# First x block in three loads, the gate row's product in bank 0, second-layer weights in three loads

## The chip, the cores and the metric

The kernel runs on one core of one Trainium2 chip. A core has a matrix engine (TensorE, PE in the profile; its weight loads are PEld), VectorE (DVE), ScalarE (ACT), GpSimd (POOL) and SyncE (SP), which here issues nearly all DMAs; sixteen DMA engines move the data. Matrix products go to PSUM, eight banks of 512 fp32 columns per partition, and are copied from there to SBUF by VectorE or ScalarE. The metric is the device time of one execution in microseconds, lower being better.

## The reference

The inputs are bf16. With S = 2048 tokens, D = 512, 32 heads of 16, and a hidden width of 1376:

```python
x = A_x
g = sigmoid((x * gate_w).sum(-1, keepdims=True))
# branch A: linear attention with softmax feature maps
q, k, v = split_heads(x @ wqkv)                    # 32 heads of 16
pq, pk = q @ w_phi[h], k @ w_phi[h]
phi = lambda p: concat([softmax(p), softmax(-p)])  # 32 features per head
kv = einsum("bhsf,bhsd->bhfd", phi(pk), v)
z  = phi(pk).sum over s
a  = ((phi(pq) @ kv) / (phi(pq) @ z + 1e-6)) @ wo
# branch B: two dense layers
b  = relu(x @ w1) @ w2
return g * a + (1 - g) * b
```

## The kernel before

**How order is made.** The program is written as one list of operations per engine (`_Plan`). Each operation may name events it waits for (`after`) and one event that it sets (`ev`); `emit` turns these into semaphore waits and increments, in the order of the list. Each engine works through its list in order. `early(eng)` marks a point in a list: what was listed before it is placed ahead of that engine's wait at the start barrier. SP's x loads, ACT's load of the gate row, DVE's two memsets and some of TensorE's warm-up products are placed so.

**Banks.** `free[bank]` holds the event that says when a PSUM bank was last read out; whoever writes the bank next waits for it. `nextbank()` deals out banks 3, 4 and 5 in turn. `gatecol` (L223) is given its bank by the caller (L562), which computes the same number as `nextbank()` would without advancing the turn.

**The start.** The first 512 tokens are loaded by `loadx0` into `XS`, four token rows per partition, so that index j = 0..3 stands for 128 tokens each. `xtr` (L235) turns 128x128 blocks (feature block dt, token block j) by a product with the identity into a PSUM bank, and `xev` (L244) copies a bank to the transposed x, `XT`, on DVE or ACT. Groups are named: a0, a1, a2 hold the feature blocks 0, 1 and 2 to 3 of the first half of the tokens, c0 and d0 feature block 0 of j = 2 and j = 3, b1 and b3 the rest of the second half. Ahead of them `warm` issues products of ones whose result nobody reads. SP then loads the first-layer weights W1 by feature block: block 0 in two pieces, blocks 1, 2 and 3 whole, and the remaining columns for all blocks (`w1r`); then the small feature-map weights, the v weights WV, and DMA transposes of the q and k weights and of the other x blocks.

`slab(t)` (L520) does feature block t of the first eight hidden units for the first 512 tokens: eight products of 512 columns, one in each PSUM bank, accumulated over the four slabs. A slab waits for its W1 piece and for the x groups that `XV[t]` names. ReLUs on ACT and DVE empty the banks. Two more hidden units (`hunit`), then `gatecol(...)`, `vtile(0)`, `vtile(1)` and the eight `pre(i)` follow, where `pre` multiplies the q and k weights with the feature map. `gatecol` transposes the gate row into a column, which DVE copies into a spare column of W1 (the event `gw`); `rest` reads that column with the last hidden units.

**The middle and the end.** For each of 16 token tiles, `atile` computes the feature map arguments, ACT the exponentials, DVE and GpSimd the normalisation; `kv` accumulates the key-value product three tiles later, and hidden units of later token blocks are put in between. The second-layer weights W2 are loaded at tile 3 (L591 to L595), on one semaphore. Afterwards, per tile, `nd` multiplies with the key-value product, `finB` (L485) does the second dense layer, `finA` the output projection, and `comb` (L508) mixes the two and stores.

Of the kernel before, what the change touches and what calls it, by code (L numbers as in the profile page):

```python
# [68 lines left out]
def bass_gated_mix__linear_kernel_hedgehog__dense_activation_relu__prompt_kernel(  # L69
# [17 lines left out]
    P = 128  # L87
# [14 lines left out]
    KU = KT - 1  # L102
    NR = DFF - KU * P

    with ExitStack() as es:
# [37 lines left out]
        XS = OT[:, 0, :].rearrange("p (j d) -> p j d", j=4)  # L143
# [7 lines left out]
        p = _Plan(["sp", "pool", "act", "dve", "pe"])  # L151
        free = {b: [] for b in range(8)}


        xq = x2[0:512, :].rearrange("(p j) d -> p j d", j=4)
        oq = o2[0:512, :].rearrange("(p j) d -> p j d", j=4)

        def orow(m):
            return oq[:, m, :] if m < 4 else o2[m * P:(m + 1) * P, :]

        def loadx0(h):
            p.dma("sp", lambda e: e.dma_start(out=XS[:, 2 * h:2 * h + 2, :], in_=xq[:, 2 * h:2 * h + 2, :]),
                  f"x0{h}", ev=f"x0{h}")

        def loadw1(t, c0=0, c1=DFF, tag=""):
            p.dma("sp", lambda e: e.dma_start(  # L166
# [2 lines left out]
        p.dma("act", lambda e: e.dma_start(out=GR[0:NDT, :], in_=gate_w.rearrange("(j p) -> j p", p=P)),  # L169
              "gr", after=["grz"], ev="gr")  # L170
        p.early("act")
        for h in range(2):
            loadx0(h)
        p.early("sp")
        loadw1(0, 0, 4 * P, "a")
# [1 line left out]
        for t in range(1, NDT):  # L177
            loadw1(t, 0, 8 * P)
        p.dma("sp", lambda e: e.dma_start(
            out=W1[:, :, 8 * P:DFF], in_=B_w1[:, 8 * P:DFF].rearrange("(j p) n -> p j n", p=P)), "w1r", ev="w1r")  # L180
        p.dma("sp", lambda e: e.dma_start(
            out=WPS[:, :, :], in_=A_w_phi.rearrange("(g hl) r c -> (hl r) g c", g=NDT)), "wps", ev="wps")
        p.dma("sp", lambda e: e.dma_start(
            out=WV[:, :, :], in_=A_wqkv[:, 2 * D:3 * D].rearrange("(j p) n -> p j n", p=P)), "wv", ev="wv")
        for i in range(2):
            p.dma("sp", lambda e, i=i: e.dma_start_transpose(
                out=WQKT[:, 4 * i:4 * i + 4, :], in_=A_wqkv[:, i * D:(i + 1) * D]), f"wqk{i}", ev=f"wqk{i}")
        for c in range(1, NCH):
            p.dma("sp", lambda e, c=c: e.dma_start_transpose(
                out=XT[:, :, c * 512:(c + 1) * 512], in_=x2[c * 512:(c + 1) * 512, :]), f"x{c}", ev=f"x{c}")  # L190
# [9 lines left out]
            after=["wps"], ev="wd")  # L200
        for gt in range(NDT):
# [4 lines left out]
                after=["wd", "m8"], ev=f"wbd{gt}")  # L206
# [5 lines left out]
             after=["iota0"], ev="idn")  # L212
        p.op("dve", lambda e: e.tensor_single_scalar(ROW8[:, :], ROW8[:, :], 4, ALU.arith_shift_right),
             after=["iota"], ev="r8")
# [3 lines left out]
             after=["r64"], ev="m32")  # L218
# [4 lines left out]
        def gatecol(bank):  # L223
            gp = PS[:, bank, 0:NDT]
            p.op("pe", lambda e: e.matmul(gp, GR[:, :], IDN[:, 0:NDT], start=True, stop=True),  # L225
                 after=["gr", "idn"] + free[bank], ev="gp")
            p.op("dve", lambda e: e.tensor_copy(W1[:, :, DFF:DFF + 1], gp.unsqueeze(2)), after=["gp"], ev="gw")  # L227
            free[bank] = ["gw"]

        def warm(n, cols=512):  # L230
            for _ in range(n):
                p.op("pe", lambda e: e.matmul(PS[:, 4, 0:cols], ones[:, 0:P], ones[:, 0:cols], start=True, stop=True),
                     after=["one"])

        def xtr(nm, js, dts, bank, last=True, off=0):  # L235
            blocks = [(dt, j) for dt in dts for j in js]
            for i, (dt, j) in enumerate(blocks):
                o = off + i * P
                p.op("pe", lambda e, dt=dt, j=j, o=o: e.matmul(
                    PS[:, bank, o:o + P], XS[:, j, dt * P:(dt + 1) * P], IDN[:, :], start=True, stop=True),  # L240
                    after=["idn", f"x0{j // 2}"] + (free[bank] if o == 0 else []),
                    ev=(f"xt{nm}" if last and i == len(blocks) - 1 else None))

        def xev(eng, nm, js, dts, bank):  # L244
            w = len(js) * P
            d = XT[:, dts[0]:dts[-1] + 1, js[0] * P:js[0] * P + w]
            s = PS[:, bank, 0:len(dts) * w].rearrange("p (t c) -> p t c", c=w)
            if eng == "dve":
                p.op("dve", lambda e: e.tensor_copy(d, s), after=[f"xt{nm}"], ev=f"xv{nm}")
            else:  # L250
                p.op("act", lambda e: e.activation(d, s, ACT.Copy), after=[f"xt{nm}"], ev=f"xv{nm}")
            free[bank] = [f"xv{nm}"]
# [12 lines left out]
        rot = [0]  # L265
# [5 lines left out]
        def hunit(c, kt, eng="act", bank=None):  # L271
            bank = nextbank() if bank is None else bank
            for t in range(NDT):
                p.op("pe", lambda e, t=t: e.matmul(  # L274
                    PS[:, bank, :], W1[:, t, kt * P:(kt + 1) * P], XT[:, t, c * 512:(c + 1) * 512],
                    start=(t == 0), stop=(t == NDT - 1)),
                    after=(xready(c) + w1all + free[bank] if t == 0 else ()),
                    ev=(f"h{c}_{kt}" if t == NDT - 1 else None))
            relu(c, kt, bank, eng)
# [123 lines left out]
        def vtile(m, eng="act", bank=2):  # L403
            b = m % VB
            for dt in range(NDT):
                p.op("pe", lambda e, dt=dt: e.matmul(  # L406
                    PS[:, bank, :], XT[:, dt, m * P:(m + 1) * P], WV[:, dt, :],
                    start=(dt == 0), stop=(dt == NDT - 1)),
                    after=((xready(m // 4) + ["wv"] + free[bank]) if dt == 0 else ()),
                    ev=(f"v{m}" if dt == NDT - 1 else None))  # L410
            dst, src = VS[:, b, :, 0:64], PS[:, bank, :].rearrange("p (g c) -> p g c", g=NG)
            after = [f"v{m}"] + ([f"kv{m - VB}"] if m >= VB else [])
            if eng == "dve":
                p.op("dve", lambda e: e.tensor_copy(dst, src), after=after, ev=f"cv{m}")
            else:
                p.op("act", lambda e: e.activation(dst, src, ACT.Copy), after=after, ev=f"cv{m}")  # L416
            free[bank] = [f"cv{m}"]

        def kv(m):
            b = m % NB  # L420
            vb = m % VB
            for g in range(NG):
                after = []
                if g == 0:
                    after = [f"pk{m}", f"cv{m}", f"one{vb}"]
                    if m == 0:
                        after += free[6] + free[7]
                p.op("pe", lambda e, g=g: e.matmul(  # L428
                    PS[:, 6 + g // 4, (g % 4) * GW:(g % 4) * GW + 65],
                    EB[:, b, 3, g * P:(g + 1) * P], VS[:, vb, g, 0:65],  # L430
                    start=(m == 0 and g % 4 == 0), stop=(m == NT - 1), skip_group_check=True),
                    after=after, ev=(f"kv{m}" if g == NG - 1 else None))
# [93 lines left out]
                    ev=(f"h0_{u}" if t == NDT - 1 else None))  # L526

        A, B = (0, 1), (2, 3)
        warm(5)
        p.early("pe")  # L530
        warm(1, 384)
        xtr("a0", A, (0,), 6)
        xtr("a1", A, (1,), 5)
        xtr("a2", A, (2,), 7, last=False)
        xtr("c0", (2,), (0,), 2)
        xtr("d0", (3,), (0,), 0)
        xtr("a2", A, (3,), 7, off=2 * P)
        xev("dve", "a0", A, (0,), 6)
        xev("act", "c0", (2,), (0,), 2)
        xev("dve", "d0", (3,), (0,), 0)  # L540
        xev("act", "a2", A, (2, 3), 7)
        xev("dve", "a1", A, (1,), 5)
        xtr("b1", B, (1, 2), 1)
        xtr("b3", B, (3,), 6)
        xev("act", "b1", B, (1, 2), 1)
        xev("dve", "b3", B, (3,), 6)
        slab(0)
# [11 lines left out]
            relu(0, u, UB[u], ("act", "dve")[u % 2])  # L559
        hunit(0, 8)  # L560
        hunit(0, 9, "dve")
        gatecol(3 + rot[0] % 3)  # L562
        vtile(0, "dve")
        vtile(1, "act", nextbank())
        for i in range(4):
# [10 lines left out]
        def unit(c, k):  # L576
            if k < 0:
                rest(c)
            else:
                hunit(c, k)  # L580

        for m in range(NT):
            atile(m)
            if m >= LAG:
                kv(m - LAG)
            if m + 3 < NT:
                vtile(m + 3)
            for u in mid[m]:
                unit(*u)
            if m == 3:  # L590
                for a, b in ((0, 4), (4, 7), (7, KU)):  # L591
                    p.dma("sp", lambda e, a=a, b=b: e.dma_start(
                        out=W2[:, a:b, :], in_=B_w2[a * P:b * P, :].rearrange("(j p) n -> p j n", p=P)),
                        "w2", ev=f"w2{a}")
                p.dma("sp", lambda e: e.dma_start(out=W2[0:NR, KU, :], in_=B_w2[KU * P:DFF, :]), "w2", ev="w2")  # L595
            if m == 5:
                for a in range(0, NDT, 2):
                    p.dma("sp", lambda e, a=a: e.dma_start(
                        out=WO[:, a:a + 2, :], in_=A_wo[a * P:(a + 2) * P, :].rearrange("(j p) n -> p j n", p=P)),
                        "wo", ev="wo" if a else None)  # L600
# [69 lines left out]
```

The softmax here doesn't subtract the row's maximum and nothing guards it: scores larger than these inputs give would overflow.

## Time and profile before

| | |
|---|---|
| median of 6 runs | 147.36 us (147.13 to 147.74) |
| the profiled execution, its own time | 147.17 us |
| its span, first to last instruction | 145.9 us |
| PE busy | 143.3 us (98%), 978 products |
| DVE busy | 92.4 us (63%) |
| ACT busy | 72.8 us (50%) |
| POOL busy | 52.1 us (36%) |
| DMA | 16.12 MB, mean 111 GB/s |

The profile page gives busy time per engine, the span in 40 slices, the DMA queues, the chain of work that ended last (followed back from the last instruction through what released each step), the costliest groups of instructions, and the DMA issues. Other views of the trace list waits by who waited for whom, one line's instructions, the instructions in order of time, and busy time within chosen stretches. An L number is a line of the kernel; times are microseconds from the start of the span unless marked ns. Products on TensorE are pipelined and their ends are modelled, so starts are the safer reading. "SPq" is SP issuing a DMA; landing is when the data's last semaphore update came.

### The profile page before, as it was taken

Reading aid. Unit: us, or ns where it says so; the run is one execution under the profiler, and the core shown is the slowest. Engines: PE = TensorE matmul, PEld = TensorE weight load, DVE = VectorE, ACT = ScalarE, POOL = GpSimd, SP = SyncE. Lnnn points to the kernel's source line nnn. Section 1 sums busy time; section 2 is a strip of 40 time slices with the busy share of each in tenths; the row PEclk is TensorE's granted clock in tenths of the full one; section 3 lists DMA queues with packets and bytes.
Section 4 is the critical chain, followed back from the end, with each engine's and each line's share of the span. In section 5 each row is a group of like instructions: output and inputs, shape, how many; then the busy total and the mean of one; then the engine's idle time right before and its main releaser. Section 6 shows DMA issues by size and latency. Waiting matters only on the chain.

```text
span 145.9 us, 2539 instructions
## 1 busy us (share of the span) xinstructions
PE 143.3 (98%) x978; PEld 72.9 (50%) x978; DVE 92.4 (63%) x158; ACT 72.8 (50%) x125; POOL 52.1 (36%) x62
## 2 busy tenths in 40 slices
PE   8999999999999999999999999999999999999994
PEld 3444754444446455544645555554444444444442
DVE  3528728777687878678698967664445555554342
ACT  3316567789778778797878862022211111111150
POOL 2022003778868678688869810200000000000000
PEclk9999999999999999999999999999999999999999
DMA  6999995113349983325834431354332223222213
GB/s 189 277 250 203 228 172 120 31 41 76 72 89 366 127 211 81 71 62 108 75 75 88 91 72 40 73 108 126 83 82 73 72 72 76 72 72 74 72 45 106
DMA packets 45221, 16.12 MB, mean 111 GB/s; under 512 B 39352, under 2 KB 44568, under 8 KB 45208
## 3 DMA queue, kind: packets, MB, share of 16 engines
q1 hardware_dynamic: 45056, 15.92, 50.2%
q8 instruction: 8, 0.13, 0.4%
q10 hardware_dynamic: 152, 0.03, 0.1%
q14 instruction: 5, 0.04, 0.1%
HBM read 4.41 MB, written 2.10 MB: 45 GB/s over the span
## 4 chain that ended last, share of the span: by engine, by line
PE 94%; DMA 3%; DVE 1%; SPq 1%; issue 0%
PE PS L485 26%; PE PS L274 19%; PE PS L330 18%; PE PS L406 10%; PE PS L494 9%; PE PS L522 4%; DMA W<-in_B_w_dram 3%; PE PS L460 3%; PE PS L428 3%; PE PS L286 2%; PE PS L308 1%; DVE WQK L508 1%; SPq L166 1%; PE PS L225 0%
## 5 line engine op out<-in xcount | busy, mean ns | idle before, releaser
L485 PE MATMUL PS<-W,HT 128*128 128x512 bf16 (+4 forms) x187 | 40.6, 366 | 0.0
L374 POOL TENSOR_TENSOR EB<-EB,SC 128x1024 bf16<-128x1024 bf16 x15 | 28.9, 1928 | 23.6 <-DVE SC L372 23.6
L350 ACT ACTIVATE EB<-PS 128x480 bf16<-128x480 f32 (+1 forms) x44 | 30.1, 756 | 14.2 <-PE PS L330 14.2
L499 ACT ACTIVATE TFA<-PS,GT 128x512 bf16<-128x512 f32 x16 | 11.0, 687 | 42.7 <-PE PS L494 36.6
L274 PE MATMUL PS<-XT,W 128*128 128x512 bf16 x128 | 30.7, 379 | 0.0
L330 PE MATMUL PS<-WQK,XT 128*128 128x480 bf16 x128 | 28.5, 366 | 0.0
L370 DVE TENSOR_REDUCE ZB<-EB 128x64 f32<-128x1024 bf16 x15 | 18.3, 1220 | 14.2 <-ACT EB L350 14.2
L508 DVE SCALAR_TENSOR_TENSOR WQK<-PS,OMG,TFA 128x512 bf16<-128x512 f32 (+2 forms) x17 | 12.2, 719 | 23.6 <-ACT TFA L499 22.4
L485 PEld LDWEIGHTS PS<-W,HT 128*128 128x128 bf16 (+1 forms) x187 | 17.0, 98 | 17.4
L260 ACT ACTIVATE HT<-PS 128x512 bf16<-128x512 f32 x35 | 20.3, 614 | 7.0 <-PE PS L522 5.1
L330 PEld LDWEIGHTS PS<-WQK,XT 128*128 128x128 bf16 x128 | 12.5, 98 | 13.6
L385 DVE TENSOR_REDUCE ZB<-EB 128x64 f32<-128x1024 bf16 x16 | 18.7, 1167 | 0.0
L274 PEld LDWEIGHTS PS<-XT,W 128*128 128x128 bf16 x128 | 12.0, 98 | 13.2
L394 POOL TENSOR_TENSOR EB<-EB,SC 128x512 bf16<-128x512 bf16 x16 | 16.9, 1058 | 1.3
L406 PE MATMUL PS<-WV,XT 128*128 128x512 bf16 x64 | 16.4, 378 | 0.0
L494 PE MATMUL PS<-WO,OT 128*128 128x512 bf16 x64 | 16.1, 378 | 0.0
L470 DVE TENSOR_TENSOR WQK<-PS,RDEN 128x512 bf16<-128x512 f32 x16 | 11.1, 691 | 0.6
L494 PEld LDWEIGHTS PS<-WO,OT 128*128 128x128 bf16 x64 | 6.1, 97 | 7.2
L416 ACT ACTIVATE VS<-PS 128x512 bf16<-128x512 f32 x14 | 8.5, 608 | 2.2 <-PE PS L406 2.2
L372 DVE RECIPROCAL SC<-ZB 128x64 f32<-128x64 f32 x16 | 8.8, 553 | 0.5
L406 PEld LDWEIGHTS PS<-WV,XT 128*128 128x128 bf16 x64 | 5.4, 97 | 5.0 <-DVE W L227 0.5
L460 PEld LDWEIGHTS PS<-KVNZ,PHQ 128*128 128x128 bf16 x128 | 6.1, 97 | 3.6
(57 smaller groups left out, 87.6 us busy)
## 6 DMA issues: line engine op xcount, KB each, us to landing
out_dram<-WQK SPq DMA_DIRECT2D x15, 128.0 KB, 1.7
W<-in_B_w_dram SPq DMA_DIRECT2D x3, 256.0 KB, 5.2
W<-in_B_w_dram SPq DMA_DIRECT2D x2, 384.0 KB, 5.5
OT<-in_A_x_dram SPq DMA_DIRECT2D x2, 256.0 KB, 2.9
WV<-in_A_wqkv_dram SPq DMA_DIRECT2D x1, 512.0 KB, 6.7
W<-in_B_w_dram SPq DMA_DIRECT2D x1, 512.0 KB, 4.3
WO<-in_A_wo_dram SPq DMA_DIRECT2D x2, 256.0 KB, 3.6
W<-in_B_w_dram SPq DMA_DIRECT2D x1, 352.0 KB, 6.2
```

The source lines that it names most:

```text
L260: p.op("act", lambda e: e.activation(dst, src, ACT.Relu), after=[f"h{c}_{kt}"], ev=ev)
L274: p.op("pe", lambda e, t=t: e.matmul(PS[:, bank, :], W1[:, t, kt * P:(kt + 1) * P], XT[:, t, c * 512:(c + 1) * 512], start=(t == 0), stop= ...
L330: p.op("pe", lambda e, dt=dt, which=which: e.matmul(PS[:, which, 0:DE], XT[:, dt, m * P:(m + 1) * P], WQK[:, which, dt * DE:(dt + 1) * DE] ...
L350: p.op("act", lambda e: e.activation(dst, s_, ACT.Exp, scale=scale), after=[f"qk{m}"] + busy, ev=ev)
L370: p.op("dve", lambda e: e.tensor_reduce(zk, ek, AX.X, ALU.add), after=[emk, f"cst{b}"], ev=f"zk{m}")
L374: p.op("pool" if m < NT - 1 else "dve", lambda e: e.tensor_tensor(EB[:, b, 3, :].rearrange("p (g f) -> p g f", f=DH), EB[:, b, 2, :].rearr ...
L385: p.op("dve", lambda e: e.tensor_reduce(ZB[:, b, 0:64].rearrange("p (h s) -> p h s", s=2), bass.AP(tensor=EB, offset=base, ap=[[EBS, P], [ ...
L394: p.op("pool", lambda e: e.tensor_tensor(EB[:, b, 0, :].rearrange("p (h s f) -> p h s f", h=H, s=2)[:, :, 1, :], EB[:, b, 1, :].rearrange( ...
L406: p.op("pe", lambda e, dt=dt: e.matmul(PS[:, bank, :], XT[:, dt, m * P:(m + 1) * P], WV[:, dt, :], start=(dt == 0), stop=(dt == NDT - 1)), ...
L485: p.op("pe", lambda e, kt=kt, M=M: e.matmul(PS[:, bank, 0:n], HT[0:M, kt, m * P:(m + 1) * P], W2[0:M, kt, cs], start=(kt == 0), stop=(kt = ...
L494: p.op("pe", lambda e, t=t: e.matmul(PS[:, bank, :], OT[:, t, m * P:(m + 1) * P], WO[:, t, :], start=(t == 0), stop=(t == NDT - 1)), after ...
L508: p.op("dve", lambda e: e.scalar_tensor_tensor(out=OSB[:, ob, cs], in0=PS[:, bank, 0:n], scalar=OMG[:, m:m + 1], in1=TFA[:, m % 2, cs], op ...
```

## The change

Four things are edited.

- The x block is loaded in three pieces in place of two: j = 0, j = 1, and j = 2 to 3 (`XJ`; `XP` maps j to its piece). All three are issued ahead of SP's wait at the start barrier.
- `xtr` takes a list of blocks. The first half's transposes are issued in two batches: feature blocks 0, 1, 2 of j = 0, then 0, 1, 2 of j = 1 with feature block 3 of both. The copies of a0 and a1 stand first in DVE's list; c0 and d0 are transposed after all of a2. The warm-up is four products of 512 columns and one of 256 ahead of the transposes, and one of 256 between j = 1 and c0; before, it was five of 512 and one of 384.
- `gatecol` uses bank 0.
- W2's first ten blocks are loaded as 5 + 5 in place of 4 + 3 + 3; the last, partial block stays a load of its own.

```diff
@@ -158,9 +158,12 @@
         def orow(m):
             return oq[:, m, :] if m < 4 else o2[m * P:(m + 1) * P, :]
 
+        XJ = ((0, 1), (1, 2), (2, 4))
+        XP = (0, 1, 2, 2)
+
         def loadx0(h):
-            p.dma("sp", lambda e: e.dma_start(out=XS[:, 2 * h:2 * h + 2, :], in_=xq[:, 2 * h:2 * h + 2, :]),
-                  f"x0{h}", ev=f"x0{h}")
+            j0, j1 = XJ[h]
+            p.dma("sp", lambda e: e.dma_start(out=XS[:, j0:j1, :], in_=xq[:, j0:j1, :]), f"x0{h}", ev=f"x0{h}")
 
         def loadw1(t, c0=0, c1=DFF, tag=""):
             p.dma("sp", lambda e: e.dma_start(
@@ -169,7 +172,7 @@
         p.dma("act", lambda e: e.dma_start(out=GR[0:NDT, :], in_=gate_w.rearrange("(j p) -> j p", p=P)),
               "gr", after=["grz"], ev="gr")
         p.early("act")
-        for h in range(2):
+        for h in range(3):
             loadx0(h)
         p.early("sp")
         loadw1(0, 0, 4 * P, "a")
@@ -232,13 +235,12 @@
                 p.op("pe", lambda e: e.matmul(PS[:, 4, 0:cols], ones[:, 0:P], ones[:, 0:cols], start=True, stop=True),
                      after=["one"])
 
-        def xtr(nm, js, dts, bank, last=True, off=0):
-            blocks = [(dt, j) for dt in dts for j in js]
+        def xtr(nm, blocks, bank, last=True, off=0):
             for i, (dt, j) in enumerate(blocks):
                 o = off + i * P
                 p.op("pe", lambda e, dt=dt, j=j, o=o: e.matmul(
                     PS[:, bank, o:o + P], XS[:, j, dt * P:(dt + 1) * P], IDN[:, :], start=True, stop=True),
-                    after=["idn", f"x0{j // 2}"] + (free[bank] if o == 0 else []),
+                    after=["idn", f"x0{XP[j]}"] + (free[bank] if o == 0 else []),
                     ev=(f"xt{nm}" if last and i == len(blocks) - 1 else None))
 
         def xev(eng, nm, js, dts, bank):
@@ -526,22 +528,25 @@
                     ev=(f"h0_{u}" if t == NDT - 1 else None))
 
         A, B = (0, 1), (2, 3)
-        warm(5)
+        warm(4)
         p.early("pe")
-        warm(1, 384)
-        xtr("a0", A, (0,), 6)
-        xtr("a1", A, (1,), 5)
-        xtr("a2", A, (2,), 7, last=False)
-        xtr("c0", (2,), (0,), 2)
-        xtr("d0", (3,), (0,), 0)
-        xtr("a2", A, (3,), 7, off=2 * P)
+        warm(1, 256)
+        xtr("a0", ((0, 0),), 6, last=False)
+        xtr("a1", ((1, 0),), 5, last=False)
+        xtr("a2", ((2, 0),), 7, last=False)
+        xtr("a0", ((0, 1),), 6, off=P)
+        xtr("a1", ((1, 1),), 5, off=P)
+        xtr("a2", ((2, 1), (3, 0), (3, 1)), 7, off=P)
+        warm(1, 256)
+        xtr("c0", ((0, 2),), 2)
+        xtr("d0", ((0, 3),), 0)
         xev("dve", "a0", A, (0,), 6)
+        xev("dve", "a1", A, (1,), 5)
         xev("act", "c0", (2,), (0,), 2)
         xev("dve", "d0", (3,), (0,), 0)
         xev("act", "a2", A, (2, 3), 7)
-        xev("dve", "a1", A, (1,), 5)
-        xtr("b1", B, (1, 2), 1)
-        xtr("b3", B, (3,), 6)
+        xtr("b1", [(dt, j) for dt in (1, 2) for j in B], 1)
+        xtr("b3", [(3, j) for j in B], 6)
         xev("act", "b1", B, (1, 2), 1)
         xev("dve", "b3", B, (3,), 6)
         slab(0)
@@ -559,7 +564,7 @@
             relu(0, u, UB[u], ("act", "dve")[u % 2])
         hunit(0, 8)
         hunit(0, 9, "dve")
-        gatecol(3 + rot[0] % 3)
+        gatecol(0)
         vtile(0, "dve")
         vtile(1, "act", nextbank())
         for i in range(4):
@@ -588,7 +593,7 @@
             for u in mid[m]:
                 unit(*u)
             if m == 3:
-                for a, b in ((0, 4), (4, 7), (7, KU)):
+                for a, b in ((0, 5), (5, KU)):
                     p.dma("sp", lambda e, a=a, b=b: e.dma_start(
                         out=W2[:, a:b, :], in_=B_w2[a * P:b * P, :].rearrange("(j p) n -> p j n", p=P)),
                         "w2", ev=f"w2{a}")
```

## The prediction

> **What bounds the kernel now.** I read the page's fourth part first: who carries the end.
>
> ```profile
> PE 94%; DMA 3%; DVE 1%; SPq 1%; issue 0%
> ```
>
> TensorE is the end, with a short piece of DMA ahead of it. The chain of waits in order of time places that piece (start, duration, what):
>
> ```profile
> 1.09 0.34 SPq L166
> ...
> 1.94 4.63 DMA W<-in_B_w_dram
> 6.57 0.05 issue
> 6.62 5.35 PE PS L522 x24
> 11.97 1.73 PE PS L274 x8
> 13.70 0.01 PE PS L225
> 13.71 1.90 PE PS L406 x8
> 15.61 0.84 PE PS L308 x16
> ```
>
> So the end hangs on one landing: the third W1 load (`loadw1(1, ...)`, issued at 1.94), which releases the second slab at 6.62. From there it is TensorE without a break. The windows view (length, then busy time of PE, PEld, DVE, ACT, POOL, clock, DMA) confirms it:
>
> ```profile
> 4.80:6.60 1.80, 1.62 (x8) 0.58 (x6) 0.85 (x10) 0.59 (x2) 0.00 (x0) 1.00 0.89 267
> 6.60:13.70 7.10, 7.08 (x34) 3.27 (x35) 3.35 (x8) 2.66 (x5) 1.73 (x5) 1.00 1.08 235
> 15.70:143.90 128.20, 128.20 (x906) 66.00 (x902) 84.25 (x126) 67.40 (x116) 49.29 (x47) 1.00 0.46 96
> ```
>
> A modelled matmul end can hide a small hole, so I compared matmul starts: after 6.62 they follow each other at 0.2155 us per 512 columns everywhere but once. The waits of the weight loads name that place, and the two before it:
>
> ```profile
> PEld PS L522 <- DMA W<-in_B_w_dram: 0.7, 1, 0.7
> PEld PS L406 <- DVE W L227: 0.5, 1, 0.5
> PEld PS L239 <- DMA OT<-in_A_x_dram: 0.2, 1, 0.2
> ```
>
> L406 is `vtile(1)`. Its first matmul starts at 14.569 where 14.211 + 0.2155 = 14.427 was possible: **0.142 us** lost, not 0.5, because weight loads run ahead. The timeline shows what it waited for, the copy of the gate column:
>
> ```profile
> 14.35 0.17 DVE L227 CAST W<-PS 128x4 bf16<-128x4 f32 x1
> 14.56 0.55 PEld L406 LDWEIGHTS PS<-WV,XT 128*128 128x128 bf16 x4 [0.47 <-DVE W L227]
> ```
>
> Last, issue to landing, for the x halves (L162, issued at 0.08 and 0.54) and the five W1 loads (L166):
>
> ```profile
> DMA to landing us min/median/max: 2.7/2.9/3.1
> DMA to landing us min/median/max: 3.3/4.6/5.5
> ```
>
> The halves land at 2.81 and 3.66. By the trace's semaphore updates the W1 loads land at 4.46, 4.81, 6.57, 7.65 and 8.35. The fourth and fifth are wanted at about 8.34 and 10.07, each a slab of 1.72 us after the one before, so they have 0.7 and 1.7 us of room.
>
> **What the Trainium skill says.** "DMA: Bandwidth & Descriptors", section "Queues, rings and completion order": each DMA engine consumes descriptors in ring order, and a load is complete only when every engine's share has landed. The trace agrees: the third W1 load's sixteen updates spread from 4.63 to 6.57, the last two at 6.39 and 6.57. Same page, "Why small descriptors are slow (HBM only)": about 3 cycles per packet on top of one per 32 bytes. By it a 1 KB packet costs (35 x 2)/67, some 4% more per byte than 2 KB; the trace's packets (about 50 ns for 1 KB, 85 to 105 for 2 KB) show no penalty. "TensorE: Matmul & The Clock Gate", "What's actually happening": TensorE runs at half clock until a window of about 3.4 us was busy. The trace agrees on the two rates (128-column transposes start 107 ns apart up to 4.07, 56 ns after); no run here shows how much idleness the window forgives.
>
> **The change, part by part.**
>
> *Gate row in bank 0.* Before, `gatecol` takes bank 3 + 2 = 5, which the next `nextbank()` hands to `vtile(1)`; that must wait for the copy ending at 14.51. Bank 0 instead: `gatecol` waits for the ReLU of unit 3, done by 12.00, well before 13.54; `vtile(1)` waits for unit 2's ReLU, over at 11.59. The copy's new waiter is `pre(0)`, first user of bank 0, at 15.44 - 0.14 = 15.30, so 0.8 us of cover. `pre(4)` wants the second wqk transpose at about 17.2; it landed at 15.91. Nothing else is near: **-0.142 us**.
>
> *Second-layer weights.* Loads of 512, 384, 384 and 96 KB become 640, 640 and 96: one issue of about 0.49 us less on SP at 42, the same bytes. They land by 49.1; the first reader is `finB(0)` at 88.2. Behind them on SP is the transpose of tile 4, wanted as a free buffer by tile 9, near 58. **0**, with 39 us of cover; uncovered it would be half a microsecond.
>
> *x in three loads.* SP issues every 0.46 us: 0.08, 0.54, and now 1.00 too. So all that follows on SP (W1, w_phi, WV, the transposes) is issued 0.46 us later. What matters is landing. One engine moves its share of a half (16 KB) in 0.7 to 0.85 us (the two halves' first updates are at 2.29 and 2.99, their last at 2.81 and 3.66). A quarter needs about 0.38, so the first lands near 2.81 - 0.38 = 2.43. The second, issue-limited, follows 0.46 later, near 2.89. The remaining half by its issue: 1.00 + 2.73 = 3.73; by data: 2.89 + 0.75 = 3.64. I take 3.75, or **+0.09** on 3.66: the rings ran short of work by about 2 x 0.08 us, part of it regained. W1 is behind x in the same rings, and there data and not issue sets the pace (five loads issued 0.47 us apart land about 0.8 apart on the quick engines). So W1 also shifts by 0.09: first load 4.55, third 6.66. Bounds: below, -0.2 (the two late engines are stragglers that could fall otherwise); above, the whole issue delay, +0.46.
>
> *TensorE ahead of it.* Four full warm matmuls and one of 256 columns end near 2.27 instead of 2.81. Three transposes of the first quarter (0.32 at half clock), five of the second by about 3.5, a 256-column warm matmul (0.21), and after the half 8 transposes where 10 stood: they end near 4.4. Before, 0.78 us passed from the half's landing to the end of the copy of d0, which the first slab needs: 3.75 + 0.78 = 4.53, so the first W1 load at 4.55 still decides, and the slab starts at 4.62, not 4.53. DVE's copy of a1 now stands ahead of d0, but its blocks are done by 3.5 and it takes 0.43, so d0 is not held. Eight matmuls: 4.62 + 1.72 = 6.35, still under 6.66. The second slab starts at 6.71 for 6.62: **+0.09 us**.
>
> Sum: -0.142 + 0.09 = **-0.05 us**. The profiled execution took 147.17 us, its span 145.9 and 1.27 around it; that becomes 147.12. The six runs' median, 147.36, lies 0.19 higher, so I say **147.31**. About 0.2% (0.29 us) is what a measurement of this kernel can tell from no change.
>
> **Rivals.**
>
> *Central, no visible change* (0.53): the sum above, or the shift between -0.15 and +0.43; 147.08 to 147.64.
>
> *The weights come late* (0.18): the late engines have no slack and the third W1 load lands 0.46 later, at 7.03. For it: the DMA share was only 0.69 at 3.2 to 3.6 us, so some engines had nothing to do just when W1 began. Against: 0.97 to 1.00 before. Slower by 0.46 - 0.14 = 0.32: 147.68. It decides from a landing past 7.00 (6.57 + 0.14 + 0.29).
>
> *The clock opens a window later* (0.07): TensorE idles about 0.7 us of the 3.4 before 4.07, where it idled 0.4. If that misses, the window of the skill's page moves the change to 7.49: the slab from 4.62 at 0.427 us has made 6.7 of 8 matmuls by then and ends at 7.77. Slower by 1.06 - 0.05: 148.4.
>
> *The first slab becomes the limit* (0.21): the third W1 load lands by 6.4 because each engine's work is smoothed, and the earlier transposes let the slab start no later than 4.53, ending at 6.26 to 6.35. Gain 0.22 to 0.36 + 0.14: about 146.95. Against: the bytes ahead of W1 are unchanged.
>
> **How the numbers follow.** Slower is the late weights, the late clock and 0.01 for the rest: 0.26. Faster 0.21, same 0.53. The range must leave out two tenths: the clock's 0.07 above, and the better part of the fastest case below, so 146.95 to 147.80. The central case's own is 147.08 to 147.64.
>
> **What would show it.** The weight loads' wait on L227 disappears and `vtile(1)` follows `vtile(0)` at 0.216 us (step one). Landings near 2.4, 2.9 and 3.75 for x, 4.55 and 6.66 for W1 (step two). The second slab's first matmul near 6.71, released by the W1 load, and TensorE unbroken after. Wrong if that start is later than 7.0, if the 128-column spacing is still 107 ns after 4.5, or if a new hole appears behind 15 us.

## The result, and the profile after

| | before | after |
|---|---|---|
| median of the runs | 147.18 us (146.68 to 148.04, 68 runs) | 147.81 us (146.96 to 149.03, 31 runs) |
| ratio, with its 95% interval | | 1.0039 (1.0026 to 1.0053) |
| the profiled execution, its own time | 147.17 us | 147.33 us |
| its span | 145.9 us | 146.0 us |

The change makes the kernel slower by 0.4%, some 0.6 us. The forecast was 0.05 us faster, inside what can be told from no change. (The ratios here leave out executions more than 1.5% above a kernel's fastest, the medians and spreads do not.) Two things stand out before any view is read: the medians differ by 0.63 us and the profiled executions by only 0.16, and the spread has grown from 1.4 to 2.1 us. The profile below is of one of the better executions of the changed kernel.

The chain of waits in order of time (start, duration, what), longest pieces alone. It now starts from an x load, where before it went through a W1 load:

```profile
0.53 2.79 DMA OT<-in_A_x_dram
5.24 7.04 PE PS L524 x32
12.28 1.73 PE PS L276 x8
14.01 1.75 PE PS L408 x8
```

All 32 products of the four slabs run as one piece. In this execution nothing waits for the third W1 load any more. The last row is the two v tiles: 1.75 us where it was 1.90, so the gate row's hole is gone.

Issue to landing, first for the three x loads, then for the five W1 loads:

```profile
DMA to landing us min/median/max: 2.4/2.8/3.2
DMA to landing us min/median/max: 2.9/3.8/4.7
```

The x pieces land at 2.46, 3.33 and **4.16** us; before, the halves landed at 2.81 and 3.66. The first and third W1 loads land at 4.56 and 6.19 (before: 4.46 and 6.57).

The timeline of TensorE at the start (start, duration, operation, tiles, count, idle before it and what ended that), first of the kernel before:

```profile
2.94 1.66 PE L239 MATMUL PS<-IDN,OT 128*128 128x128 bf16 x16
4.53 1.89 PE L522 MATMUL PS<-XT,W 128*128 128x512 bf16 x8
```

and of the changed kernel:

```profile
2.60 0.48 PE L241 MATMUL PS<-IDN,OT 128*128 128x128 bf16 x3
3.37 0.71 PE L241 MATMUL PS<-IDN,OT 128*128 128x128 bf16 x5 [0.29 <-DMA OT<-in_A_x_dram]
3.88 0.42 PE L235 MATMUL PS<-ONE 128*128 128x256 bf16 x1
4.21 1.03 PE L241 MATMUL PS<-IDN,OT 128*128 128x128 bf16 x8
5.03 0.77 PE L524 MATMUL PS<-XT,W 128*128 128x512 bf16 x2
```

The last transpose of the three at 2.60 starts at 2.765 and would be followed at 2.87; the next one starts at 3.37, so TensorE lost 0.50 us there, plus 0.32 before the first transpose and 0.11 before the half. The 8 transposes from 4.21 start 107 ns apart, the spacing of half clock, where before they had reached 56 ns by then. The first slab starts at 5.03 (before 4.53), the second at 6.935 (before 6.620): 0.315 later. Behind the second v tile the distance is 0.161, so the gate's bank gave back 0.154. That is the whole difference of this execution, 0.16 us. Past the slabs TensorE is unbroken:

```profile
4.80:6.60 1.80, 1.80 (x12) 0.94 (x10) 0.89 (x10) 0.98 (x3) 0.00 (x0) 1.00 0.96 268
6.60:13.70 7.10, 7.10 (x35) 3.21 (x34) 3.57 (x9) 2.59 (x5) 1.73 (x5) 1.00 1.04 237
15.70:143.90 128.20, 128.20 (x908) 66.12 (x905) 84.11 (x126) 67.46 (x116) 49.31 (x47) 1.00 0.44 96
```

What is left to explain is the rest of the 0.63, which this execution does not show.

### The profile page after: what moved, and what is told of

Read it like the earlier page. It is cut to its first block, busy times and chain, and to the rows that moved or that the text cites. A ratio compares the mean times of both kernels' runs of the same rounds, so it can differ in the third digit from the quotient of the medians.

```text
span 146.0 us, 2539 instructions
## 1 busy us (share of the span) xinstructions
PE 143.3 (98%) x978; PEld 73.2 (50%) x978; DVE 92.5 (63%) x158; ACT 72.7 (50%) x125; POOL 52.1 (36%) x62
## 3 DMA queue, kind: packets, MB, share of 16 engines
HBM read 4.41 MB, written 2.10 MB: 45 GB/s over the span
## 4 chain that ended last, share of the span: by engine, by line
PE 96%; DMA 2%; DVE 1%; SPq 0%; issue 0%
PE PS L487 26%; PE PS L276 19%; PE PS L332 18%; PE PS L496 9%; PE PS L408 9%; PE PS L524 5%; PE PS L462 3%; PE PS L430 3%; DMA OT<-in_A_x_dram 2%; PE PS L288 2%; PE PS L310 1%; PE PS L241 1%; DVE WQK L510 1%; SPq L166 0%; PE PS L235 0%
```

## The experiments

Two theories. **Late x**: SP's third x issue brings the last x piece half a microsecond later, and the first slab with it. **Late clock**: the new holes in TensorE's work keep the early clock windows (the stretches of about 3.4 us of the prediction) from counting as busy, so that TensorE comes to full clock later, in some executions much later. Each kernel ran with the kernel before on the same chip; medians are compared within a session.

### The parts alone

**The gate's bank (e1_gate).**

```diff
-        gatecol(3 + rot[0] % 3)
+        gatecol(0)
```

> The kernel before with one edit: the gate row's product goes to bank 0. Every theory here agrees that the hole of 0.142 us ahead of the second v tile closes and nothing takes its place: 0.10 to 0.17 us faster in the median, and the spread of the runs stays as it was (about 1.4 us from the lowest to the highest). If it is not faster, the copy of the gate column has only changed the place where it holds TensorE up.

146.89 us (146.40 to 147.65) against 147.05: ratio 0.9991 (0.9976 to 1.0006). The size is the expected one, though the interval also holds no change. Its trace has the copy of the gate column (L227), and weight loads that no longer wait for it:

```profile
13.35 1.20 PEld L406 LDWEIGHTS PS<-WV,XT 128*128 128x128 bf16 x7
14.16 0.17 DVE L227 CAST W<-PS 128x4 bf16<-128x4 f32 x1
```

**The second-layer loads (e6_w2).**

```diff
-                for a, b in ((0, 4), (4, 7), (7, KU)):
+                for a, b in ((0, 5), (5, KU)):
```

> The kernel before with the second-layer weights loaded as 5 + 5 blocks and nothing else. Theories late clock and late x both expect no change, within 0.1 us, because TensorE runs unbroken past these loads. If they are the missing cost, this is slower by 0.3 to 0.5 us.

147.09 us against 147.12: 0.9999 (0.9980 to 1.0018). Nothing waits for the two loads, which land 4.8 and 6.0 us after issue at 42. No cost of this part shows.

**The x part alone (e2_x, and again e10_x_again).** The changed kernel with both of the above put back.

> The changed kernel with the gate's bank and the second-layer loads put back, so the x part alone. If the bank was a gain of 0.15 us in the changed kernel and the second-layer loads were nothing, this is slower than before by 0.6 + 0.15, some 0.7 to 0.85 us. If the second-layer loads or the bank cost something there, it is slower by 0.6 us or less.

147.35 us (147.03 to 149.10) against 147.05: 1.0024 (1.0008 to 1.0041).

> The x part alone a second time, since its 0.3 us does not add up with the gate's gain to the 0.6 us of the whole change. If parts add, it comes out 0.5 to 0.8 us slower than before; if again near 0.3 us, with the half landing near 3.87 where the whole change has it near 4.18, the rest lies in where the loads land and not in the clock.

147.55 us (146.96 to 148.31) against 147.14: 1.0035 (1.0016 to 1.0054). Both intervals lie above 1: the x part is the slow one. Its 0.30 and 0.41 us don't add up with the gate's gain to the whole change's 0.6. But where the loads land differs between the sessions. The half landed at 3.87 in the first and 4.41 in the second, which has the larger loss. Neither of the outcomes named for the second run came: the parts still don't add, and the half did not land early again.

**The whole change once more (e5_again).**

> The changed kernel itself once more, beside its parts. Alone, the x part came out 0.3 us slower than before, the whole change 0.6 us slower in its own measurement, though the gate's bank alone was 0.1 to 0.2 us faster. If the parts add up, the change is here 0.1 to 0.3 us slower than before; if it is again 0.6 us or more, the parts do not add, or the second-layer loads cost what is missing. Theory late clock expects single executions to lie as far up as 1.8 us above the fastest.

147.72 us (146.99 to 149.25) against 147.12: 1.0045 (1.0022 to 1.0067). The parts' sum of 0.1 to 0.3 us did not come; the loss of 0.6 us repeated, and with it executions 2 us above the fastest. Its profile fell on a long execution, 148.68 us, and is the clearest evidence, because its x loads land where those of the first profile did (2.50, 3.32, 4.20) and the first slab starts at 5.07 for 5.03. Yet its second slab starts at 8.28 for 6.94. The windows view from 6 to 8 us (length, PE busy, and in brackets the number of products) of the changed kernel in its first profile, then in this one:

```profile
6.00:8.00 2.00, 2.00 (x11) 0.88 (x9) 0.47 (x3) 0.00 (x0) 0.00 (x0) 1.00 0.95 244
```

```profile
6.00:8.00 2.00, 2.00 (x6) 0.68 (x5) 0.51 (x4) 0.00 (x0) 0.00 (x0) 1.00 1.00 276
```

TensorE looks fully busy in both. But 11 products overlap the first stretch, and 6 the second. In the second profile the products start 0.427 us apart up to 8.06, 0.216 after. The clock column reads 1.00 all the while and doesn't tell; the count does. The same program with the same landings, 1.35 us apart in time, 1.34 us apart at the second slab: what differs is when full clock came, near 5.4 (from the spacing) or at 8.06 (from the trace's record of the clock).

### Late clock

**Holes in the kernel before (e4_holes).**

```diff
-        warm(5)
+        warm(4)
         p.early("pe")
-        warm(1, 384)
+        warm(1, 256)
```

> The kernel before with the changed kernel's shorter warm-up (four products of 512 columns and one of 256 in place of five and one of 384) and nothing else, which leaves TensorE idle for half a microsecond before the first transpose. Theory late clock: slower than before by 0.2 to 0.5 us, with a longer tail of slow executions. Theory late x: no change within 0.1 us, since the first transpose waits for its x piece either way.

147.46 us (146.74 to 149.22) against 147.05: 1.0020 (1.0000 to 1.0040), the median 0.41 higher. Its x halves land where they always did (2.74 and 3.60), so this is not late x. Ten of 22 executions lie at 147.1 or under, no slower than before, and the ratio's interval touches no change; but six are longer than the longest of 75 of the kernel before (147.96), up to 149.22. The profiled one, 148.99 us, has full clock from 8.60:

```profile
2.87 2.03 PE L239 MATMUL PS<-IDN,OT 128*128 128x128 bf16 x16 [0.39 <-DMA OT<-in_A_x_dram]
4.88 4.37 PE L522 MATMUL PS<-XT,W 128*128 128x512 bf16 x11
```

Eleven products of the slabs in 4.37 us. Taking away unread warm-up work and nothing else gave the kernel the long tail.

**The holes filled (e3_fill, and again e11_fill_again).** The changed kernel with

```diff
         p.early("pe")
-        warm(1, 256)
+        warm(1, 384)
...
         xtr("a2", ((2, 0),), 7, last=False)
+        warm(1, 384)
         xtr("a0", ((0, 1),), 6, off=P)
```

> The changed kernel with TensorE's two long waits for the x pieces filled with warm-up products (384 columns in place of 256 before the first transpose, 384 more between the first and second piece). Theory late clock: the change is slow because these holes keep the clock window from counting as busy, so that full clock comes later in many executions; then the median falls by 0.3 to 0.6 us against the changed kernel and the highest run comes down from 149.0 to near 148. Theory late x: the change is slow because the last x piece lands half a microsecond later and the first slab with it; then filling holes gives nothing, within 0.1 us of the changed kernel.

147.19 us (146.89 to 147.82) against 147.05: 1.0009 (0.9995 to 1.0023).

> The changed kernel with the holes filled a second time, beside the x part alone. Theory late clock: again within 0.3 us of before and no execution above 148; full clock in the profile between 3.4 and 6.8 us, one window's length from the first busy window's end. If the first result was luck of the phase, executions near 149 appear.

147.30 us (146.99 to 147.95) against 147.14: 1.0011 (0.9994 to 1.0028). The losses of 0.14 and 0.16 us stand against the whole change's 0.60, and no execution of either is above 148. TensorE from 2 to 5 us in the first of them:

```profile
2.58 0.48 PE L241 MATMUL PS<-IDN,OT 128*128 128x128 bf16 x3
2.86 0.52 PE L235 MATMUL PS<-ONE 128*128 128x384 bf16 x1
3.18 0.64 PE L241 MATMUL PS<-IDN,OT 128*128 128x128 bf16 x5
3.65 0.27 PE L235 MATMUL PS<-ONE 128*128 128x256 bf16 x1
3.89 0.62 PE L241 MATMUL PS<-IDN,OT 128*128 128x128 bf16 x8
```

Full clock comes at 3.58 in this profile and 3.68 in the second. In the second the half landed at 4.14, as late as in the changed kernel. So two parts are apart here. With the holes filled the change costs 0.14 to 0.16 us net (each interval by itself still holds no change), about 0.3 with the gate's gain of 0.15 taken out; the holes cost the other 0.45.

What is left comes, in these profiles, through W1. The head of the chain in the first filled profile:

```profile
2.42 4.12 DMA W<-in_B_w_dram
6.58 4.06 PE PS L524 x18
```

In both filled profiles the first slab is through before the third W1 load, issued at 2.42 in place of 1.94, has landed (6.54 and 6.82), and the second slab starts right after that landing, at 6.58 and 6.87 (6.62 before the change). So with the holes filled, the delay by SP's third x issue shows at the second slab through the late weights, a rival of the prediction.

### Late x

**The second piece issued by ACT, holes filled (e7_actq).** `loadx0` takes the issuing engine as an argument, and to e3_fill is added

```diff
+        loadx0(1, "act")
         p.dma("act", lambda e: e.dma_start(out=GR[0:NDT, :], ...
...
-        for h in range(3):
+        for h in (0, 2):
             loadx0(h)
```

> The kernel with the filled holes, and the second x piece issued by ACT ahead of the gate row, so that SP issues the first quarter at 0.08, the half at 0.54 and W1 from 1.09 as before the change. Theory late x: what remained of the loss with filled holes (0.14 us over before, some 0.3 us with the gate's gain taken out) is the SP issue of the third piece; the half lands near 3.65 in place of 3.85, and the median falls by 0.15 to 0.3 us against the filled kernel. Theory late clock alone: no change against the filled kernel, within 0.1 us.

147.09 us against 147.12: 0.9998 (0.9979 to 1.0017), one execution of 189 us left aside. The half lands at 3.64 and the first and third W1 loads at 4.02 and 5.56. Against the filled kernel's +0.14 and +0.16 us this is 0.17 to 0.19 better, the size that late x expected, though the intervals overlap. The edit brings W1 forward together with the half, and these two profiles put the gain on W1: the first slab starts at 4.60 where it started at 4.61 in the first filled profile, and the second, which no longer waits, at 6.32 for 6.58.

**The second piece issued by ACT, holes left (e9_holes_act).** The same edit to the changed kernel, nothing else.

> The changed kernel with its holes as they are, and the second x piece issued by ACT, so that the half and W1 are issued as early as before the change. It separates the two causes: the filled kernel took away the holes and kept the late half, this one keeps the holes and takes the late half away. If late x is worth 0.15 us and late clock the rest, it is 0.3 to 0.5 us slower than before. If the holes matter mostly because the late half makes them long, it is within 0.2 us of before. The highest executions stay near 149 if the first hole alone, 0.3 us before the first transpose, can spoil a clock window.

146.94 us (146.56 to 147.75) against 147.14: 0.9999 (0.9978 to 1.0020). Of the two outcomes that I had named, 0.3 to 0.5 us slower did not come; within 0.2 us of before did, and no execution is near 149. The interval lies below the whole change's (1.0022 to 1.0067), if only just. The trace shows what changed:

```profile
2.64 1.01 PE L242 MATMUL PS<-IDN,OT 128*128 128x128 bf16 x8 [0.15 <-DMA OT<-in_A_x_dram]
3.44 0.42 PE L236 MATMUL PS<-ONE 128*128 128x256 bf16 x1
3.77 1.04 PE L242 MATMUL PS<-IDN,OT 128*128 128x128 bf16 x8
```

The second quarter now lands at 2.81, in time for TensorE to run its eight transposes without a break. The half lands at 3.72. The largest hole, the 0.50 us, was itself made by the late second quarter. So one cause stands behind the losses: the three x pieces queued one behind another on SP, with W1 behind them.

### Versions that might beat both

**The kernel before with the gate's bank and its own holes filled (e8_gate_fill).** To e1_gate are added `warm(1, 512)` for `warm(1, 384)` and `warm(1, 192)` ahead of the second half's first transpose.

> The kernel before with the gate row's product in bank 0 and its own two small holes ahead of full clock filled: 512 columns in place of 384 before the first transpose, 192 columns before the second half. Theory late clock: the early windows count as busy even more often, so the upper executions come down and the median is 0.2 to 0.4 us below before. If the holes of before were too small to matter, only the gate's 0.1 to 0.17 us is gained.

146.98 us (146.50 to 147.68) against 147.12: 0.9992 (0.9977 to 1.0006). No more than the gate's gain; filling the small holes of before shows no gain of its own.

**The changed kernel with ACT's issue and the two remaining holes filled (e12_best).** To e9_holes_act, 384 for 256 columns in both one-product warm-ups.

> The changed kernel with the second x piece issued by ACT, and the two waits that are left filled: 384 columns of warm-up ahead of the first transpose and 384 ahead of the half, none between the quarters. Late x gone, holes gone, gate's gain kept: 0.15 to 0.35 us faster than before, no execution above 147.9. If the kernel with ACT's issue and the holes left in was already free of the late clock, it is no faster than that one, 0.1 to 0.2 us below before.

146.99 us (146.49 to 147.77) against 147.08: 0.9992 (0.9970 to 1.0014). In its profile full clock comes at 3.27 and the second slab starts at 6.125, the earliest of all, with a span of 145.2 us; the median, 0.09 us lower, shows no more than the gate's gain and not the 0.15 to 0.35 us expected. No kernel tried is faster than before beyond its interval.

## Why the prediction was wrong

*The gate's bank, -0.142 us.* Right. The trace shows 0.154 us gained at that place, nothing took its place, and alone the median fell by 0.16, though that interval also holds no change.

*The second-layer loads, 0.* Right within what can be told: 0.9999 (0.9980 to 1.0018).

*The x loads: the half at 3.75.* **This is the first step that failed.** I estimated "1.00 + 2.73 = 3.73" with the time from issue to landing of the first half, which had no load ahead of it. The right row was the second half's, 0.54 to 3.66 or 3.13 us: 0.99 + 3.13 = 4.12. Measured were 4.16 and 4.20 in the two profiles of the changed kernel, 3.85 to 4.41 over the six profiles of kernels that issue all three on SP. The second quarter, put at 2.89, landed at 3.33 and 3.32 (2.93 to 3.33 over the six). I had both rows and averaged the difference away by saying that data, not issue, sets the pace. A smaller slip is in the reading of the packets: in the profile before the median packet took 46 ns for 1 KB and 84 for 2 KB, some 10% more per byte, where I read no penalty; for a quarter's eight packets on an engine that is an estimated 0.03 us, too little to explain the half.

*W1 shifts by 0.09 and still decides.* The first W1 load landed at 4.56 and 4.57, as predicted. The third, put at 6.66, landed at 6.19 and 6.21. But neither decided in these two profiles. The slabs waited for x and for TensorE: "the slab starts at 4.62" became 5.03, and the transposes' "they end near 4.4" became 5.03, because the half came 0.41 us later than put and all eight after it ran at half clock. The rival of the late weights did not decide here, but it did where the holes were filled: there the third W1 load, at 6.54 and 6.82, released the second slab. The 0.46 us of issue delay hit x first and W1 behind it.

*The clock.* I held the late clock at 0.07 and priced it at 1.06 us when it hits. It is the larger part of the loss. The idle time that I counted, 0.7 us of the 3.4, was too low, with the second quarter put 0.44 us too early: it was 0.97, namely 0.35 + 0.46 + 0.16 in the profile that came to full clock at 8.06. What I missed in principle is that the clock window is not fixed to the start of the program. I read one profile, in which full clock came at 4.07, as the kernel's property. The Trainium skill, "TensorE: Matmul & The Clock Gate", section "What's actually happening", calls the window free-running, and the traces agree: full clock begins at 3.27, 3.58, 3.64, 3.68, 4.07, 8.06 and 8.60 in the profiles whose record has it, and lasts 143.36 us (42 windows of 3.413) in the early ones, 139.946 (41) in the two late ones. The other seven profiles have no such record; by the spacing of their starts they come to full clock between about 4.2 and 6.6 us. One of them is e6_w2, which up to 40 us is the kernel before: it comes to full clock near 6.07, in an execution of 147.62 us. So the kernel before has later executions too, and the one that I had was an early one. The median over many executions then depends on how often an early window fails to count as busy, and a hole that the profiled execution gets away with still costs. Priced for the mean execution and not as an accident, the step would have moved the forecast to the slower side.

*The size when it hits* was under-estimated too: 1.06 us predicted, from 4.07 to 7.49, against 1.34 us between the two profiles of the changed kernel, from 5.4 to 8.06.

*The range*, 146.95 to 147.80, missed 147.81 narrowly, but it was built around a median of 147.36 from six runs where 68 give 147.18; the forecast change was -0.05 us and the measured one +0.63.

What stays open. First, how much idle time a window forgives: windows with 0.96 us idle (e4_holes) and 0.97 us (e5_again), 28% of 3.413, failed, and windows with clearly less passed, but one with 0.93 us seems to have passed in the first profile of the changed kernel, where the clock has no record and I went by spacing. If there is a limit, it lies near these values; three windows do not fix it. Second, the x part alone measured 0.30 and 0.41 us where the whole change and the gate's gain ask for about 0.75; the intervals overlap only in part (up to 1.0054 for the x part, and 1.0022 at least for the whole change, to which the gate's 0.0009 is to be added), and the scatter of the landings between sessions may be the rest. That wasn't settled. Third, the share of x and of W1 in what remains with the holes filled: no run moved the one without the other.

## What to carry to other kernels

A load split in two lands its first part sooner, but every later part on the same queue is one issue later (here 0.46 us), so take issue to landing from the row of a load in the same place in the queue. Warm-up products whose result nobody reads are part of the timing: where TensorE waits in place of such products, full clock may come later, and filling the waits again took the loss back here (0.45 of 0.6 us). And when a spread grows more than a median, look at which executions the profile did not show.

## What the runs showed of the hardware

- Full clock came anywhere from 3.27 to 8.60 us after the start, and where the trace records it, it lasted a whole number of windows of 3.413 us (143.36 and 139.946 us). Taking 0.53 us (640 columns at half clock) of unread warm-up products out of the kernel before raised its median by 0.41 us and its slowest execution from 147.96 to 149.22, with full clock at 8.60 in the profile.
- The trace's clock column stayed at 1.00 while products of 512 columns started 0.427 us apart. The number of products in a stretch, or the spacing of their starts, shows half clock; the busy share and that column don't.
- A load issued by ACT did not hold up SP's: with the second quarter on ACT at 0.21, all three x pieces were in by 3.72 and 3.64 (4.16 and 4.20 with all three on SP), and the first W1 load by 4.47 and 4.02 (4.46 before the change).
